# Linear attention and SwiGLU, forward and backward, on one core: a rebuilt k/q stage, six residual buffers and a bank-wise emptied dm step

## Chip, cores, metric

One core of one Trainium2 chip. The metric is device time in microseconds (us) of one execution of the whole kernel. The kernel before takes 821.44 us (median of 3 runs, 821.32 to 822.36).

Engines: PE is TensorE (matmuls), DVE is VectorE, ACT is ScalarE, POOL is GpSimd, SP issues most of the transfers. PE writes its results into the memory PSUM, and DVE or ACT copy them out. A *PSUM tile* is what the kernel allocates there at once; here each covers two *banks*. It is not to be confused with a tile of 128 rows. *By starts* means that a late start is measured as the start of an instruction less the end of PE's earlier work, counted with the usual distance from start to start (0.1355 us for a matmul of 320 columns).

## The reference, cut

```python
def _A_ref(x, wqkv, wo):                       # linear attention, 32 heads of 20
    q, k, v = ...                              # x @ wqkv, S = 2048, D = 640
    phi = lambda t: jnp.where(t > 0, t + 1, jnp.exp(t)) + 1e-6
    pq, pk = phi(q), phi(k)
    kv = jnp.einsum("bhsd,bhse->bhde", pk, v)
    z = jnp.einsum("bhsd->bhd", pk)
    ...                                        # o = (pq kv) / (pq z + 1e-6)
    return o @ wo
h = x + _A_ref(_layernorm(x), wqkv, wo)
h2 = h + (silu(_layernorm(h) @ w_gate) * (_layernorm(h) @ w_up)) @ w_down
# returned: h2 and the gradients of all inputs for a given grad_out
```

S is worked in 16 tiles of 128 rows. Three places matter here. The **k/q stage** (about 0 to 55 us) normalises each tile of x, transposes it on PE, multiplies by the k and q weights and forms phi. The **stage before h1** (about 85 to 100 us) builds W2, the product of the kv state with wo, and fills idle places of PE with "dm steps" (grad_out times the transposed w_down). The **h1 stage** (about 100 to 149 us) alternates products ps_a with dm steps; DVE adds x to ps_a. Names in the profile: xn is the normalised x and xnT its transposed copy, wqk are the k and q weights, rstd is the inverse root of the variance, ps_... are PSUM tiles, dm and dmst are the buffers into which ACT empties the dm steps, and ring is a buffer that transfers fill with dq and dk in the backward part.

## The kernel before, where the change touches it

```python
    def ln1(t):                                     # one tile: normalise, transpose, copy
        ...                                         # xn[:, t] on DVE (only centred for t < 2)
        tp = psum.tile([P, D], BF16, name="ps_t", tag="mm")
        for kt in range(DT):
            nc.tensor.transpose(tp[:, kt * P:(kt + 1) * P], xn[:, t, kt * P:(kt + 1) * P], ident[:])
        tpv = tp[:].rearrange("p (k c) -> p k c", c=P)
        if t == 0:
            wait_for(nc.scalar.copy(out=xnT[:, t, 0:3], in_=tpv[:, 0:3]), load_3())
            nc.scalar.copy(out=xnT[:, t, 3:5], in_=tpv[:, 3:5])
        else:
            nc.scalar.copy(out=xnT[:, t], in_=tpv)
    ...
    with tc.manual_schedule(engines={EngineType.PE, EngineType.DVE, EngineType.Activation}):
        ...
        warm(31)                                    # dummy matmuls until x lands
        ln1_stats(0)
        ...
        warm(12)
        ...
            if t + 2 < ST:                          # statistics two tiles ahead
                ln1_stats(t + 2)
                ln1_rstd(t + 2)                     # POOL: an addition and a power
        ...
    # the dm step: ten matmuls into both banks of one PSUM tile, one copy of both
                ps = mm("ps_dm")
                dm_mm(ps, wdT3 if g == 3 else wdT, t, g)
                dst = dmst[:, t // 2] if g == 3 else dm_t[g][:, t:t + 2, :]
                nc.scalar.copy(out=dst[:, :, :w], in_=ps[:, :, :w])
    ...
    # the stage before h1
        dm(1)
        for i in range(DT):
            if i == 3:
                dm(1)
            ps = mm("ps_w2t")
            mm_heads(ps, ...)
            nc.scalar.copy(out=half(W2T[:, i, :]), in_=row(ps))
            nc.sync.dma_start_transpose(out=W2[:, :, i * P:(i + 1) * P], in_=W2T[:, i, :])
        ...
        dm(3)
    # the h1 stage
        for t in range(ST + 2):
            if t < ST:
                xr = xrs.pop(t)                     # one of five buffers, loaded about two tiles ahead
                ps = mm("ps_a")
                mm_row(ps, ..., W2, ...)
                nc.vector.tensor_tensor(out=half(xr[:]), in0=row(ps), in1=half(xr[:]), op=ALU.add)
                ...
                dm(1)
            if t > 0:
                load_xr(t + 2)
            ...
            nc.scalar.dma_start(out=scr_h1_v[:, u, :], in_=h1[:])
```

`mm(name)` hands out one of four PSUM tiles, each of two banks. `manual_schedule` keeps the program's order on the engines that it names; POOL was not among them.

## Time and profile before

| | before |
|---|---|
| time, median (runs) | 821.44 us (3) |
| span of the profiled run | 819.0 us |
| PE busy | 812.0 us, 99% |
| first x lands (first statistics on DVE) | 3.62 us |
| tile 4's transposes | 18.31 us |
| z sums (end of the k/q stage) | 55.72 us |
| a dm step, and the one after it | 89.06, 92.10 us |
| first gate product pg (end of the h1 stage) | 149.12 us |

The table gives places on the time axis and not busy shares, because PE is busy almost all the time. A change can win only where PE's next instruction starts later than the one before it allows. The lines are in the prediction below.

### The profile page before, as it was taken

The page shows a single profiled execution, that of the slowest core. Times are in us where ns is not written, and L with a number is a line of the kernel's source. Part 1 is how long each engine was busy: PE and PEld are TensorE (multiplying, and loading weights), DVE is VectorE, ACT ScalarE, POOL GpSimd, SP SyncE. Part 2 cuts the span into 40 slices and gives each one's busy share as a digit, 9 for nine tenths or more (in the row PEclk, how much of TensorE's full clock was granted, in tenths as well). Part 3 has the DMA queues.
Part 4 walks back from the last instruction along what each step waited for, and adds up shares of the span by engine and source line. Part 5 has one row for each costly group of instructions (what it writes and reads, how often), then busy time and mean ns, then how long its engine had stood idle before and what let it go on. Part 6 is the DMA issues. An engine that isn't in the chain of part 4 may idle for free.

```text
span 819.0 us, 14057 instructions
## 1 busy us (share of the span) xinstructions
PE 812.0 (99%) x5540; PEld 521.7 (64%) x5540; DVE 442.4 (54%) x874; ACT 291.0 (36%) x412; POOL 188.2 (23%) x345
## 2 busy tenths in 40 slices
PE   8999999999999999999999999999999999999998
PEld 6776656555555555555566677777777777777675
DVE  6878676891077018810660147787793366631212
ACT  6982422770084126500741122322322133322010
POOL 3330022322412312221125301211220111112330
PEclk9999999999999999999999999999999999999999
DMA  9994589999759997894498757977498999999962
GB/s 301 195 356 86 140 175 280 244 226 214 198 123 206 208 207 178 183 249 115 98 233 185 258 123 217 219 206 181 110 224 178 172 174 165 176 204 259 227 177 75
DMA packets 278321, 158.61 MB, mean 194 GB/s; under 512 B 235052, under 2 KB 264877, under 8 KB 278256
## 3 DMA queue, kind: packets, MB, share of 16 engines
q1 hardware_dynamic: 251696, 82.12, 53.1%
q0 software_dynamic: 17744, 64.45, 26.6%
q10 hardware_dynamic: 8816, 11.16, 4.3%
q8 instruction: 43, 0.70, 0.4%
q14 instruction: 22, 0.18, 0.1%
HBM read 47.68 MB, written 53.66 MB: 124 GB/s over the span
## 4 chain that ended last, share of the span: by engine, by line
PE 92%; DVE 4%; ACT 2%; DMA 1%; issue 1%; POOL 0%; DVEq 0%; ACTq 0%
PE ps_dw L627 21%; PE ps_dhn L109 14%; PE ps_dxn L871 8%; PE ps_o L932 7%; PE pu L563 7%; PE pg L558 7%; PE ps_dwqk L109 5%; PE ps_dm L385 5%; PE ps_y L109 3%; PE ps_dp L109 3%; PE ps_dk L109 3%; PE ps_gt L678 3%; PE ps_a L109 3%; PE pdm L385 2%; DVE st L134 1%; ACT phi_e L307 1%
## 5 line engine op out<-in xcount | busy, mean ns | idle before, releaser
L109 PE MATMUL ps_dhn<-wgT,cols 128*128 128x320 bf16 x864 | 119.5, 299 | 0.0
L627 PE MATMUL ps_dw<-dd,hn 128*128 128x448 bf16 (+1 forms) x640 | 118.8, 346 | 0.0
L109 PEld LDWEIGHTS <-cols 128*128 128x128 bf16 x864 | 84.5, 98 | 32.9
L627 PEld LDWEIGHTS <-hn 128*128 128x128 bf16 x640 | 62.6, 98 | 54.2
L629 DVE CAST dwev<-ps_dw 128x896 bf16<-128x896 f32 (+3 forms) x12 | 10.9, 908 | 123.5 <-PE ps_dw L627 123.5
L629 ACT CAST dwev<-ps_dw 128x896 bf16<-128x896 f32 (+1 forms) x20 | 17.6, 878 | 157.9 <-PE ps_dw L627 146.7
L592 POOL DMA_DIRECT2D scr_dT<-stg x64 | 34.8, 543 | 168.7 <-DMA stg<-dd 163.2
L147 DVE CUSTOM_DVE_ANT_0 lb_a<-lb_dy,hn 128x640 bf16<-128x640 bf16 x32 | 26.4, 826 | 75.3 <-ACT lb_dy L145 75.3
L558 PE MATMUL pg<-wgu,hnT 128*128 128x448 bf16 (+1 forms) x320 | 63.6, 346 | 0.0
L563 PE MATMUL pu<-wgu,hnT 128*128 128x448 bf16 (+1 forms) x320 | 63.6, 346 | 0.0
L932 PE MATMUL ps_o<-wd,mT 128*128 128x320 bf16 (+3 forms) x462 | 61.3, 295 | 0.0
L627 PE MATMUL ps_dw<-m_s,dh 128*128 128x448 bf16 (+1 forms) x320 | 60.4, 346 | 0.0
L871 PEld LDWEIGHTS <-ring 128*128 128x128 bf16 x480 | 47.0, 98 | 18.2
L932 PEld LDWEIGHTS <-mT 128*128 128x128 bf16 (+1 forms) x462 | 41.8, 97 | 17.6 <-issue 2.6
L871 PE MATMUL ps_dxn<-wqkvT,ring 128*128 128x320 bf16 x320 | 51.3, 299 | 0.0
L563 PEld LDWEIGHTS <-hnT 128*128 128x128 bf16 x320 | 31.3, 98 | 27.1
L627 PEld LDWEIGHTS <-dh 128*128 128x128 bf16 x320 | 31.3, 98 | 27.1
L558 PEld LDWEIGHTS <-hnT 128*128 128x128 bf16 x320 | 31.3, 98 | 27.0
L298 PE MATMUL ps_kq<-wqk,xnT 128*128 128x320 bf16 x320 | 46.4, 299 | 1.4 <-ACT xnT L290 1.4
L385 PEld LDWEIGHTS <-dh2T 128*128 128x128 bf16 x320 | 31.1, 98 | 25.8 <-issue 0.9
L385 PE MATMUL ps_dm<-wdT,dh2T 128*128 128x448 bf16 (+1 forms) x240 | 46.8, 344 | 0.6 <-ACT dmst L399 0.5
L145 ACT ACTIVATE lb_dy<-ps_dhn,rstd 128x640 bf16<-128x640 f32 x16 | 12.7, 793 | 87.8 <-PE ps_dhn L109 87.8
(162 smaller groups left out, 1277.8 us busy)
## 6 DMA issues: line engine op xcount, KB each, us to landing
scr_dT<-stg POOLq DMA_DIRECT2D x48, 224.0 KB, 3.0
cols<-scr_dT POOLq DMA_DIRECT2D x6, 1728.0 KB, 8.1
scr_m<-m_s POOLq DMA_DIRECT2D x12, 448.0 KB, 4.4
cols<-scr_dT ACTq DMA_DIRECT2D x2, 1728.0 KB, 9.5
out_dram<-dwev POOLq DMA_DIRECT2D x30, 112.0 KB, 3.3
scr_dT<-stg POOLq DMA_DIRECT2D x16, 192.0 KB, 2.6
scr_pk<-pk SPq DMA_DIRECT2D x4, 640.0 KB, 7.5
scr_pq<-pqa SPq DMA_DIRECT2D x4, 640.0 KB, 7.8
```

The lines of the kernel that those rows point to most:

```text
L109: nc.tensor.matmul(ps[:, ci, :320], lhsT=lhs(k), rhs=rhs(k, *NCH[ci]), start=(start and k == 0), stop=(stop and k == n - 1))
L147: nc.vector.tensor_tensor_reduce(out=a[:], in0=dy[:], in1=xhat, scale=1.0, scalar=0.0, op0=ALU.mult, op1=ALU.add, accum_out=sums[:, 1:2])
L298: nc.tensor.matmul(ps[:, ci, :320], lhsT=xnT[:, t, k, :], rhs=wqk[:, k, w0 + n0:w0 + n1], start=(k == 0), stop=(k == DT - 1))
L385: nc.tensor.matmul(ps[:, c, :w], lhsT=dh2T[:, kt, (t + c) * P:(t + c + 1) * P], rhs=wdT[:, kt, o:o + w], start=(kt == 0), stop=(kt == DT - 1))
L558: nc.tensor.matmul(pg[:, c, :w], lhsT=hnT[:, kt, (t + c) * P:(t + c + 1) * P], rhs=wg[:, kt, 0:w], start=(kt == 0), stop=(kt == DT - 1))
L563: nc.tensor.matmul(pu[:, c, :w], lhsT=hnT[:, kt, (t + c) * P:(t + c + 1) * P], rhs=wg[:, kt, w:2 * w], start=(kt == 0), stop=(kt == DT - 1))
L592: nc.gpsimd.dma_start(out=scr_dT[t + c, :, KO[g]:KO[g] + GK[g], :], in_=stg[:, :GK[g], :])
L627: nc.tensor.matmul(ps[:, c, :w], lhsT=lhs(t), rhs=rhs(t), start=(t == 0), stop=(t == ST - 1))
L629: copy(out=ev[:, :len(parts), :w], in_=ps[:, :len(parts), :w])
L678: nc.tensor.matmul(ps[:, ci, :320], lhsT=dh1[:, t, i * P:(i + 1) * P], rhs=pqs_tm[:, t, n0:n1], start=(t == 0), stop=(t == ST - 1))
L871: nc.tensor.matmul(ps[:, ci, :320], lhsT=lhs[:, i, :], rhs=rhs[:, i, n0:n1], start=(k == 0 and i == 0), stop=(k == 2 and i == DT - 1))
L932: nc.tensor.matmul(po(t, ci), lhsT=mTs[t // 4][r, t % 4, j, :], rhs=wd[r, j, n0:n1], start=(t, ci) not in opened, stop=last)
```

## The change

The intent is to take away PE's remaining pauses: POOL's order and ACT's load at the start of the k/q stage, one wait for a PSUM buffer before h1, and late x in the h1 stage. The core of the diff, with cuts marked:

```diff
-    work = ctx.enter_context(tc.tile_pool(name="work", bufs=5))
+    work = ctx.enter_context(tc.tile_pool(name="work", bufs=6))
...
+    NC = 3
+    BY_V = (1, 2, 3, 6, 9, 12)          # tiles whose transposes DVE copies instead of ACT
...
+    def ln1_tr(t):                       # tiles 0 and 1: three transposes in one bank, two in the other
+        tp = psum.tile([P, 2, 2 * 512], BF16, name="ps_t", tag="mm")
+        for c, (k0, k1) in enumerate(((0, 3), (3, DT))):
+            for kt in range(k0, k1):
+                nc.tensor.transpose(tp[:, c, (kt - k0) * P:(kt - k0 + 1) * P], ...)
+        return [...]                     # one piece per bank
...
+        nc.scalar.activation(out=half(dst[:, t, :]), ..., func=ACT.Exp, scale=sc)
+        nc.scalar.activation(out=half(rr[...]), ..., func=ACT.Relu, scale=sc)
...
+    def phi(which, t, n=2):              # two tiles in one DVE operation
...
-    with tc.manual_schedule(engines={EngineType.PE, EngineType.DVE, EngineType.Activation}):
+    with tc.manual_schedule(engines={EngineType.PE, EngineType.DVE, EngineType.Activation, EngineType.Pool}):
...
+        ln1_centre(0, 0, 3 * P)          # first tile in pieces
+        ln1_centre(0, 3 * P, D)
+        copies(0, nc.scalar.copy)
+        warm(8)
...
+            kq_mm(t, 0, (lambda: copy1(t + 1)) if t + 1 < ST else None)
             if t == 2:
+                ln1_stats(4)
+                ln1_stats(5)
...
-                dm_mm(ps, wdT3 if g == 3 else wdT, t, g)
-                nc.scalar.copy(out=dst[:, :, :w], in_=ps[:, :, :w])
+                if g == 0 and t == 8:    # a copy after each half of the matmuls
+                    dm_mm(ps, wdT, t, g, lambda c: nc.scalar.copy(out=dst[:, c, :w], in_=ps[:, c, :w]))
+                else:
+                    dm_mm(ps, wdT3 if g == 3 else wdT, t, g)
+                    nc.scalar.copy(out=dst[:, :, :w], in_=ps[:, :, :w])
...
-        for t in range(3):
+        for t in range(6):
             load_xr(t)
...
-            if t > 0:
-                load_xr(t + 2)
+            if t > 2:
+                load_xr(t + 3)
```

More of the change, by code (lines that the diff above doesn't have):

```diff
@@ L174 @@
     wpool = wB.enter_context(tc.tile_pool(name="wpool", bufs=2))
+    fA = ExitStack()
+    rr = fA.enter_context(tc.tile_pool(name="fA", bufs=1)).tile([P, 4, 2, D], BF16, name="rr")
     def fw(name):
-        return wpool.tile([P, 2, GM], BF16, name=name, tag="f", bufs=6)
+        return fpool.tile([P, 2, GM], BF16, name=name, tag="f")
     def load_wgu(g):
@@ L258, with ln1_centre @@
     pqa = big.tile([P, ST, D], BF16, name="pqa", tag="B")
-    ers = {}
-    NC = 2
+    NC = 3
+    BY_V = (1, 2, 3, 6, 9, 12)
     def ln1_stats(t):
-        st = ln_stats(x_tm[t // 8][:, t % 8, :], mv1[:, t, :])
-        if t == 0:
-            wait_for(st, load_2())
+        st6 = small.tile([P, 2, 6], FP32, name="st6", tag="st6")
+        for ci, (n0, n1) in enumerate(NCH):
+            st = nc.vector.bn_stats(out=st6[:, ci, :], in_=x_tm[t // 8][:, t % 8, n0:n1])
+            if t == 0 and ci == 0:
+                wait_for(st, load_2())
+        nc.vector.bn_aggr(out=mv1[:, t, :], in_=st6[:].rearrange("p a b -> p (a b)"))
+        ln_rstd(mv1[:, t:t + 1, :], rstd1, t, 1)
+    def ln1_centre(t, c0=0, c1=D):
+        nc.vector.tensor_scalar(out=xn[:, t, c0:c1], in0=x_tm[t // 8][:, t % 8, c0:c1], scalar1=mv1[:, t, 0:1],
+                                scalar2=None, op0=ALU.subtract)
     def ln1_xn(t):
@@ L271, in ln1_xn, with ln1_tr1 @@
                                 scalar2=rstd1[:, t:t + 1], op0=ALU.subtract, op1=ALU.mult)
-    def ln1_rstd(t):
-        ln_rstd(mv1[:, t:t + 1, :], rstd1, t, 1)
-    def ln1(t):
-        if t < NC:
-            nc.vector.tensor_scalar(out=xn[:, t, :], in0=x_tm[t // 8][:, t % 8, :], scalar1=mv1[:, t, 0:1],
-                                    scalar2=None, op0=ALU.subtract)
-        else:
-            ln1_xn(t)
+    def ln1_tr(t):
+        tp = psum.tile([P, 2, 2 * 512], BF16, name="ps_t", tag="mm")
+        for c, (k0, k1) in enumerate(((0, 3), (3, DT))):
+            for kt in range(k0, k1):
+                nc.tensor.transpose(tp[:, c, (kt - k0) * P:(kt - k0 + 1) * P], xn[:, t, kt * P:(kt + 1) * P], ident[:])
+        return [(slice(k0, k1), tp[:, c, :(k1 - k0) * P].rearrange("p (k c) -> p k c", c=P))
+                for c, (k0, k1) in enumerate(((0, 3), (3, DT)))]
+    def ln1_tr1(t):
         tp = psum.tile([P, D], BF16, name="ps_t", tag="mm")
@@ L284, in ln1, with kq_mm @@
             nc.tensor.transpose(tp[:, kt * P:(kt + 1) * P], xn[:, t, kt * P:(kt + 1) * P], ident[:])
-        tpv = tp[:].rearrange("p (k c) -> p k c", c=P)
-        if t == 0:
-            wait_for(nc.scalar.copy(out=xnT[:, t, 0:3], in_=tpv[:, 0:3]), load_3())
-            nc.scalar.copy(out=xnT[:, t, 3:5], in_=tpv[:, 3:5])
-        else:
-            nc.scalar.copy(out=xnT[:, t], in_=tpv)
-    def kq_mm(t, which, between=None):
+        return tp[:].rearrange("p (k c) -> p k c", c=P)
+    def kq_mm(t, which, between=None, pieces=((0, DT),)):
         dst, w0 = ((pk, D), (pqa, 0))[which]
         ps = mm("ps_kq")
-        for k0, k1 in ((0, 3), (3, DT)) if t == 0 else ((0, DT),):
+        for k0, k1 in pieces:
             for ci, (n0, n1) in enumerate(NCH):
@@ L299, in kq_mm @@
                                      start=(k == 0), stop=(k == DT - 1))
-            if between and (t > 0 or k0 == 0):
+            if between and k0 == 0:
                 between()
-        def act():
-            e = fw("phi_e")
-            r = fw("phi_r")
-            sc = rstd1[:, t:t + 1] if t < NC else 1.0
-            nc.scalar.activation(out=e[:, :, :320], in_=row(ps), func=ACT.Exp, scale=sc)
-            nc.scalar.activation(out=r[:, :, :320], in_=row(ps), func=ACT.Relu, scale=sc)
-            ers.setdefault(t, []).append((dst, e, r))
@@ L311, in kq_mm @@
-        return act
-    def kq_phi(t, last=True):
-        n = len(ers[t]) if last else 1
-        for _ in range(n):
-            dst, e, r = ers[t].pop(0)
-            nc.vector.tensor_scalar(out=e[:, :, :320], in0=e[:, :, :320], scalar1=1.0, scalar2=1e-6,
-                                    op0=ALU.min, op1=ALU.add)
-            nc.vector.tensor_tensor(out=half(dst[:, t, :]), in0=e[:, :, :320], in1=r[:, :, :320], op=ALU.add)
-        if last and t % 4 == 3:
-            sl = slice(t - 3, t + 1)
-            nc.sync.dma_start(out=scr_pk_v[:, sl, :], in_=pk[:, sl, :])
-            nc.sync.dma_start(out=scr_pq_v[:, sl, :], in_=pqa[:, sl, :])
-            nc.sync.dma_start(out=scr_xnT[sl].rearrange("t p k c -> p t k c"), in_=xnT[:, sl])
@@ L326 @@
-    with tc.manual_schedule(engines={EngineType.PE, EngineType.DVE, EngineType.Activation}):
+        sc = rstd1[:, t:t + 1] if t < NC else 1.0
+        nc.scalar.activation(out=half(dst[:, t, :]), in_=row(ps), func=ACT.Exp, scale=sc)
+        nc.scalar.activation(out=half(rr[:, 2 * which + t // 2 % 2, t % 2, :]), in_=row(ps), func=ACT.Relu, scale=sc)
+    def phi(which, t, n=2):
+        e = (pk, pqa)[which][:, t:t + n, :]
+        nc.vector.tensor_scalar(out=e, in0=e, scalar1=1.0, scalar2=1e-6, op0=ALU.min, op1=ALU.add)
+        nc.vector.tensor_tensor(out=e, in0=e, in1=rr[:, 2 * which + t // 2 % 2, t % 2:t % 2 + n, :], op=ALU.add)
+        if (t + n) % 4 == 0:
+            sl = slice(t + n - 4, t + n)
+            if which == 0:
+                nc.sync.dma_start(out=scr_pk_v[:, sl, :], in_=pk[:, sl, :])
+            else:
+                nc.sync.dma_start(out=scr_pq_v[:, sl, :], in_=pqa[:, sl, :])
+                nc.sync.dma_start(out=scr_xnT[sl].rearrange("t p k c -> p t k c"), in_=xnT[:, sl])
@@ L328 @@
+    PIECES = ((0, 3), (3, DT))
+    with tc.manual_schedule(engines={EngineType.PE, EngineType.DVE, EngineType.Activation, EngineType.Pool}):
         ps = mm("ps_warm")
@@ L332, in warm, with copies, copy1 @@
                 nc.tensor.matmul(ps[:, 0, :P], lhsT=ident[:], rhs=ident[:], start=True, stop=True)
+        def copies(t, eng_copy):
+            for sl, src in ln1_tr(t):
+                c = eng_copy(out=xnT[:, t, sl], in_=src)
+                if t == 0 and sl.start == 0:
+                    wait_for(c, load_3())
+        def copy1(t):
+            (nc.vector.tensor_copy if t in BY_V else nc.scalar.copy)(out=xnT[:, t], in_=ln1_tr1(t))
         warm(31)
         ln1_stats(0)
-        ln1_rstd(0)
@@ L337 @@
-        ln1(0)
-        warm(12)
+        ln1_centre(0, 0, 3 * P)
+        ln1_centre(0, 3 * P, D)
+        copies(0, nc.scalar.copy)
+        warm(8)
         ln1_stats(1)
-        ln1_rstd(1)
-        kq_mm(0, 0, lambda: ln1(1))()
+        ln1_centre(1)
+        kq_mm(0, 0, lambda: copies(1, nc.vector.tensor_copy), PIECES)
         ln1_stats(2)
-        ln1_rstd(2)
-        kq_mm(1, 0)()
-        kq_mm(0, 1)()
-        for t in range(1, ST):
-            if t == 1:
-                ln1(2)
-            if t > 1:
-                kq_mm(t, 0, (lambda: ln1(t + 1)) if t + 1 < ST else None)()
-            if t == 2:
-                kq_phi(0)
-            if t + 2 < ST:
-                ln1_stats(t + 2)
-                ln1_rstd(t + 2)
-            if t == 1:
-                kq_phi(0, last=False)
-            kq_mm(t, 1)()
-            if t > 1:
-                kq_phi(t - 1)
-            if t >= ST - NC:
-                ln1_xn(t - ST + NC)
@@ L363 @@
-        kq_phi(ST - 1)
+        ln1_centre(2)
+        kq_mm(1, 0, None, PIECES)
+        ln1_stats(3)
+        kq_mm(0, 1, lambda: copy1(2), PIECES)
+        phi(0, 0)
+        ln1_xn(3)
+        kq_mm(1, 1)
+        for t in range(2, ST):
+            if t > 3 and t + 3 < ST:
+                ln1_stats(t + 3)
+            kq_mm(t, 0, (lambda: copy1(t + 1)) if t + 1 < ST else None)
+            if t == 2:
+                ln1_stats(4)
+                ln1_stats(5)
+            if t == 3:
+                ln1_stats(6)
+            if t == ST - 1:
+                phi(0, t - 1, 1)
+            kq_mm(t, 1)
+            if t == 3:
+                phi(1, 0)
+            elif t == ST - 1:
+                phi(0, t, 1)
+                phi(1, t - 3)
+                phi(1, t - 1)
+            elif t > 3:
+                phi(t % 2, t - 2 - t % 2)
+            if t + 2 < ST:
+                ln1_xn(t + 2)
+            if ST - NC - 1 <= t < ST - 1:
+                ln1_xn(t - ST + NC + 1)
@@ L375, with dm_mm @@
         ps_z = mm("ps_zb")
+    fA.close()
+    fpool = wB.enter_context(tc.tile_pool(name="fpool", bufs=6))
     dm_t = {0: strips.tile([P, ST, GM], BF16, name="dm0", tag="S")}
-    def dm_mm(ps, wdT, t, g):
+    def dm_mm(ps, wdT, t, g, each=None):
         w = GW[g]
@@ L386, in dm_mm @@
                                  rhs=wdT[:, kt, o:o + w], start=(kt == 0), stop=(kt == DT - 1))
+            if each:
+                each(c)
     def dm_steps():
@@ L396, in dm_steps @@
                 ps = mm("ps_dm")
-                dm_mm(ps, wdT3 if g == 3 else wdT, t, g)
                 dst = dmst[:, t // 2] if g == 3 else dm_t[g][:, t:t + 2, :]
-                nc.scalar.copy(out=dst[:, :, :w], in_=ps[:, :, :w])
+                if g == 0 and t == 8:
+                    dm_mm(ps, wdT, t, g, lambda c: nc.scalar.copy(out=dst[:, c, :w], in_=ps[:, c, :w]))
+                else:
+                    dm_mm(ps, wdT3 if g == 3 else wdT, t, g)
+                    nc.scalar.copy(out=dst[:, :, :w], in_=ps[:, :, :w])
                 if g == 3:
```

## The prediction

> **What bounds the kernel now.** I read the page first, then who waited for whom on TensorE (PE), then the timelines of the engines by start times over the first 150 us.
>
> Page, parts 1 and 4 (chain of waits):
>
> ```profile
> span 819.0 us, 14057 instructions
> PE 812.0 (99%) x5540; PEld 521.7 (64%) x5540; DVE 442.4 (54%) x874; ACT 291.0 (36%) x412; POOL 188.2 (23%) x345
> ...
> PE 92%; DVE 4%; ACT 2%; DMA 1%; issue 1%; POOL 0%; DVEq 0%; ACTq 0%
> ```
>
> PE is busy 812.0 of 819.0 us. The change removes no matmul that counts (four warm-up ones), so it can only win the time in which PE stands still. Who PE waited for:
>
> ```profile
> PE ps_warm L332 <- POOL ident masks.py:199: 1.4, 1, 1.4
> PE ps_kq L298 <- ACT xnT L290: 1.4, 2, 1.1
> PE ps_dm L385 <- ACT dmst L399: 0.5, 1, 0.5
> PE ps_t L284 <- DVE xn L278: 0.3, 1, 0.3
> PE ps_z L370 <- DVE pk L319: 0.2, 1, 0.2
> ```
>
> 3.8 us in all, 1.4 of it the preamble, which stays. The ends of matmuls are modelled (a matmul of 320 columns is shown as 299 ns, yet the next one starts after 135), so gaps under about 0.16 us are hidden and shown gaps are that much too short. I therefore measure gaps from start to start. The PE timeline of the k/q stage:
>
> ```profile
> 6.25 0.99 PE L298 MATMUL ps_kq<-wqk,xnT 128*128 128x320 bf16 x6
> 7.08 0.44 PE L284 MATMUL ps_t<-ident,xn 128*128 128x128 bf16 x5
> 7.36 0.71 PE L298 MATMUL ps_kq<-wqk,xnT 128*128 128x320 bf16 x4
> 8.31 2.89 PE L298 MATMUL ps_kq<-wqk,xnT 128*128 128x320 bf16 x20 [0.24 <-ACT xnT L290]
> 11.03 0.44 PE L284 MATMUL ps_t<-ident,xn 128*128 128x128 bf16 x5
> 11.31 1.52 PE L298 MATMUL ps_kq<-wqk,xnT 128*128 128x320 bf16 x10
> 13.95 1.53 PE L298 MATMUL ps_kq<-wqk,xnT 128*128 128x320 bf16 x10 [1.12 <-ACT xnT L290]
> 15.32 0.44 PE L284 MATMUL ps_t<-ident,xn 128*128 128x128 bf16 x5
> 15.60 2.88 PE L298 MATMUL ps_kq<-wqk,xnT 128*128 128x320 bf16 x20
> 18.31 0.44 PE L284 MATMUL ps_t<-ident,xn 128*128 128x128 bf16 x5
> ```
>
> From 15.60 to 18.31 are 20 matmuls: 135.5 ns each. Five transposes take 0.28. A tile so costs PE 2.99 us, and from 15.32 to 51.27 the transposes repeat every 2.99 to 3.00 us: **PE never waits in the steady part**. The trap is that ScalarE (ACT) shows no idle time there either (five operations, starts 3.00 us apart from tile to tile), and VectorE (DVE) needs 3.01 us per tile. Three engines are matched, and the chain of waits names ACT's phi_e and phi_r. Lightening ACT and DVE cannot shorten a stage whose PE work already lies end to end. What is open is the start: 7.36 + 4 x 0.1355 = 7.90 to 8.31 is 0.41, and 11.31 + 1.355 = 12.67 to 13.95 is 1.28. The cause of both shows on POOL and ACT:
>
> ```profile
> 8.49 1.62 POOL L140 TENSOR_TENSOR rstd<-lnv,nhalf 128x1 f32<-128x1 f32 x3
> 9.10 0.79 ACT L307 ACTIVATE phi_e<-ps_kq,rstd 128x640 bf16<-128x640 f32 x1 [0.85 <-POOL rstd L140]
> 13.17 0.72 ACT L290 COPY xnT<-ps_t 128x640 bf16<-128x640 bf16 x1
> ```
>
> POOL did the additions of tiles 0, 1 and 2 before its first power, so the first phi began at 9.10 though its matmuls were done at about 7.9; ACT never caught up, and the copy of tile 2 went behind six phi operations at 13.17.
>
> Two later places, same method. In the stage before h1, PE's w2t products end at 90.95 + 21 x 0.043 = 91.85 (0.043 from 14 of them between 93.99 and 94.59) and the next dm step starts at 92.10: 0.25. In the stage of ps_a and dm, a ps_a product starts 0.19 late at 116.71, and the dm step at 137.19 comes 0.70 after 135.14 + 1.355. There DVE waits for x:
>
> ```profile
> 115.83 0.82 DVE L513 TENSOR_TENSOR xr<-ps_a,xr 128x640 bf16<-128x640 f32 x1 [3.62 <-DMA xr<-in_A_x_dram]
> 127.19 0.82 DVE L513 TENSOR_TENSOR xr<-ps_a,xr 128x640 bf16<-128x640 f32 x1 [2.43 <-DMA xr<-in_A_x_dram]
> 136.34 0.80 ACT L399 CAST dmst<-ps_dm 128x768 bf16<-128x768 f32 x1 [4.33 <-DVE hn L530]
> ```
>
> Late x makes DVE late; ACT issues the h1 stores in order, stands behind them, and empties dm late.
>
> **What the Trainium skill says.** (1) "Trainium Kernel Development and Optimization", Performance Expectations: matmul busy time is a bad metric since matmuls are pipelined. The trace agrees: 299 ns shown against 135.5 from start to start. (2) "TensorE: Matmul & The Clock Gate", "Wait — 56ns, not 53.3ns?": a warm matmul takes N / 2.4 GHz plus about 2.5 ns, which is 135.8 for 320 columns and 55.8 for 128. Measured 135.5 and 56: PE is at its floor. (3) "VectorE: DVE Perf Modes", the errata section's table and "Why PSUM operands drop a tier": a copy out of PSUM costs 120 + FD/Accel cycles at 0.96 GHz, with at most two elements a cycle for 16-bit data. I estimate 0.46 us for 640 elements, 0.33 for 384 and 0.26 for 256. The trace of before has no such copy; fp32 ones of 896 elements on DVE take 0.91 to 1.09, in keeping with one element a cycle. (4) "PSUM — Partial Sum Buffer", PSUM bank collisions: guard PSUM by bank. Splitting the transposes, and the dm step, over two banks lets the first bank be read while PE writes the second.
>
> **The change, part by part.** I walked the new program order through the four engines with the durations above (DVE: statistics 0.92 + 0.13, centring 0.30, normalising 0.36 from start to start; ACT with a per-row scale 0.68 an operation, without 0.59; from the start of the aggregate to a usable rstd 1.46, as at 11.41 to 12.87).
>
> *First tile in pieces.* DVE centres 384 columns in about 0.22 instead of 640 in 0.30, so the transposes start near 5.10 instead of 5.23; ACT's copy waits for three of them, not five (0.11). First k matmul at 6.0 instead of 6.25: gain 0.24. The next x and the q weights are asked for after the first half of the statistics, about 0.65 earlier, so weights (3.8 us to landing) are there by 8.4, before the 9.0 at which q starts.
>
> *Order of POOL, copies on DVE.* POOL in program order has rstd of tile 0 by about 6.2. Phi of tile 0 starts when its matmuls end, near 7.9. DVE's two copies of tile 1 (7.2 to 7.8) let k of tile 1 follow at 7.66 without the gap of 0.41. Then q of tile 0 from 9.0, q of tile 1 from 10.7, k of tile 2 from 12.0: the gap of 1.28 is gone too, since DVE copied tile 2 at 10.3. So far PE is 0.24 + 0.41 + 1.28 = 1.9 ahead: tile 4's transposes would be due at 16.4, not 18.31.
>
> *Statistics ahead: a new wait.* The program puts the statistics of tiles 4 and 5 behind the DVE copy of tile 3, which has to await tile 3's transposes (13.4 + 0.5). Copy to 14.25, statistics 4: aggregate starts at 15.17, statistics 5 to 16.35, rstd of tile 4 at 15.17 + 1.46 = 16.63, and PE sees xn about 0.45 later, at 17.1. PE was ready at 16.4. So I expect one new wait of about 0.7, on tile 4's transposes, which gives back a third: **net gain of the start 1.2**. Later the tiles clear by 0.4 us or more each, since joint phi (about 1.29 for two tiles against 2 x 0.79 = 1.58) brings DVE under 2.7 us a tile.
>
> *Six copies on DVE (3.5 us of ACT) and joint phi (0.15 us of DVE per tile):* beside PE's work; worth 0 in the steady part. The end of the stage stays: phi of tile 15 waits for ACT's relu, and 0.2 stays on the z sums.
>
> *dm step by bank:* the first half is copied while PE fills the second; the buffer is free about 0.36 before 92.06. Gain 0.25, all of that gap.
>
> *Six x buffers:* tiles 3 to 5 are loaded before the SP queue is taken by the transposes of pq (until 112.6), later ones three tiles ahead, some 6 to 9 us against a landing of 3.2 (at most 6.4). Both gaps go: 0.19 + 0.70 = 0.89; I book 0.85.
>
> Sum 1.2 + 0.25 + 0.85 = **2.3 us** (the roundings taken together). After 150 us PE lies end to end, so the gain should reach the end undiminished: 821.44 - 2.3 = 819.1 us.
>
> **Rivals.** (A) *ACT is the bound of the k/q stage*, as its unbroken row and the chain's phi_e and phi_r suggest. Six copies of 0.59 gone would then shorten the stage by 3.5 us in place of 1.2, and the kernel would land near 816.8. Against it: PE's 135.5 ns and 2.99 us a tile leave nothing to take. (B) *No new wait on tile 4*: if rstd or DVE's copies are quicker than I reckon, the start yields its full 1.9 and the kernel lands at 818.4. For it: POOL's power varies from 0.54 to 0.82 us. (C) *The freed waits come back as others*: a queue of transfers that is nearly full from 120 to 180 us (mean share 1.07 or more) could make x late in spite of its third tile of lead, or the tracking of the one shared buffer of relu results could tie ACT's writes to DVE's reads. Then only 0.5 to 1 us is left, 820.5 or more. Against it: the k/q stage's buffers are reused after four tiles, and x moves out of the crowded stretch.
>
> **Range and chances.** The start between 0.6 and 1.9, dm 0.1 to 0.25, x 0.4 to 0.9; with B and the good ends 818.3, with the bad ends 820.3. Runs of before spread by 1 us. Range 818.0 to 820.4, centre 819.1. 2% is 16 us, more than twice all idle time of PE, so faster by over 2% gets 0.01; slower would need a wait of 16 us, 0.01.
>
> **What would show it.** In the changed profile: first k matmul near 6.0; no ACT-caused gap before 14; a PE wait on xn of tile 4 of about 0.7 near 17; transposes 2.99 us apart after it; tile 15's z sums about 1.2 earlier; the dm step right behind the w2t products; no DVE wait for x above 1 us and no late start of PE between 100 and 148. Wrong would be: a shorter period than 2.99 (rival A), no wait at 17 (B), or new gaps after 20 us (C).

## The result

The kernel after takes **820.23 us** (median of 4 runs, 819.70 to 820.97) against 821.38 in the same session (4 runs, 821.25 to 822.36). The ratio is 0.9984 with a 95% interval of 0.9967 to 1.0001. Ratios here are the mean time of one kernel's runs over that of the other's of the same rounds, so not quite the ratio of the medians quoted. The gain is about 1.15 us where 2.3 was predicted. The interval just includes 1, so these eight runs alone do not show a gain clear of noise; the repeat e12 below, with 0.9988 [0.9976, 1.0000], points the same way. The class "within 2%" and the range 818.0 to 820.4 held.

Page of the kernel after, parts 1 and 4:

```profile
span 817.9 us, 13973 instructions
PE 811.4 (99%) x5536; PEld 521.1 (64%) x5536; DVE 443.5 (54%) x853; ACT 288.9 (35%) x407; POOL 191.5 (23%) x345
...
PE 97%; ACT 1%; DVE 1%; DMA 0%; issue 0%; DVEq 0%
```

The span fell by 1.1 us and the chain of waits now runs over PE for 97% where it had 92%. Who PE waited for, after (columns: us in total, times, longest):

```profile
PE ps_warm L330 <- POOL ident masks.py:199: 1.4, 1, 1.4
PE ps_t L286 <- DVE xn L275: 0.7, 1, 0.7
PE ps_dm L406 <- ACT dm L422: 0.6, 1, 0.6
PE ps_t L293 <- DVE xn L279: 0.3, 1, 0.3
PE ps_z L388 <- DVE pk L313: 0.2, 1, 0.2
```

The two waits of the first lines of the k/q stage (ps_kq for ACT's xnT, 1.4 us) and the one on dmst are gone. Two are new: a dm step waits for ACT's copy of its own first half (L422 is the new bank-wise copy), and transposes wait for xn (L279 is the normalising). The start of PE's timeline shows the latter (columns: start, duration, engine, line, operation, count, idle time shown before it and its releaser):

```profile
7.48 2.96 PE L302 MATMUL ps_kq<-wqk,xnT 128*128 128x320 bf16 x20
10.28 0.44 PE L293 MATMUL ps_t<-ident,xn 128*128 128x128 bf16 x5
10.72 3.51 PE L302 MATMUL ps_kq<-wqk,xnT 128*128 128x320 bf16 x24
14.06 0.44 PE L293 MATMUL ps_t<-ident,xn 128*128 128x128 bf16 x5
14.34 2.88 PE L302 MATMUL ps_kq<-wqk,xnT 128*128 128x320 bf16 x20
17.57 0.45 PE L293 MATMUL ps_t<-ident,xn 128*128 128x128 bf16 x5 [0.35 <-DVE xn L279]
```

By the starts of the single matmuls the gap of 0.41 is down to 0.07 (before tile 1's k, at 8.10), and the one of 1.28 is gone. From 14.34 twenty matmuls last to 14.34 + 20 x 0.1355 = 17.05, but tile 4's transposes start at 17.57: a new wait of 0.52. DVE's timeline shows why:

```profile
14.55 0.49 DVE L339 COPY xnT<-ps_t 128x640 bf16<-128x640 bf16 x1 [1.55 <-PE ps_t L293]
14.95 0.88 DVE L268 BATCH_NORM_STATS2 st<-x_tm 128x6 f32<-128x320 bf16 x2
...
17.07 0.45 DVE L279 TENSOR_SCALAR xn<-x_tm,mv,rstd 128x640 bf16<-128x640 bf16 x1
```

DVE stood idle 1.55 us for tile 3's transposes before it could start the statistics of tile 4, as the prediction walked it. From tile 5 on the period is 2.99 to 3.00 us, as before.

The stage before h1, PE, in the kernel before:

```profile
89.06 2.05 PE L385 MATMUL ps_dm<-wdT,dh2T 128*128 128x448 bf16 x10
...
92.10 2.05 PE L385 MATMUL ps_dm<-wdT,dh2T 128*128 128x448 bf16 x10
```

and after, PE and then the first of ACT's two copies:

```profile
88.33 1.10 PE L406 MATMUL ps_dm<-wdT,dh2T 128*128 128x448 bf16 x5
90.05 1.11 PE L406 MATMUL ps_dm<-wdT,dh2T 128*128 128x448 bf16 x5 [0.62 <-ACT dm L422]
91.00 1.04 PE L128 MATMUL ps_w2t<-yk,wvo 128*128 128x120 bf16 x21
91.89 2.05 PE L406 MATMUL ps_dm<-wdT,dh2T 128*128 128x448 bf16 x10
```

```profile
89.47 0.53 ACT L422 CAST dm<-ps_dm 128x448 bf16<-128x448 f32 x1 [1.58 <-PE ps_dm L406]
```

The first five matmuls (0.19 each, from ten of them between 89.06 and 90.95 before) are issued by 89.28. The second five start at 90.05, right after ACT's copy of the first half ended at 90.00. PE lost 0.77 in the middle of the step. The aim of the change was met all the same: the next dm step comes right after the w2t products (91.00 + 21 x 0.043 = 91.90). From one dm step to the next it took 3.04 before and 3.56 after.

In the h1 stage DVE no longer waits for x at all (7.8 us in four waits before). Its wait on the adding of x is now for PE:

```profile
DVE xr L539 <- PE ps_a L109: 9.2, 12, 0.9
```

From the dm step at 92.10 (91.89 after) to the first gate product at 149.12 (148.02) it took 57.02 before and 56.13 after: 0.89 gained.

The sum, in this pair of traces: start of the k/q stage +0.74 (z sums at 54.98, not 55.72), dm step -0.52, h1 stage +0.89, together 1.11, which is the difference of the spans. Behind 149 us everything is shifted by that amount.

### The profile page after: what moved, and what is told of

It is laid out like the page before. It is cut to its first block, busy times and chain, and to the rows that moved or that the text cites. A ratio compares the mean times of both kernels' runs of the same rounds, so it can differ in the third digit from the quotient of the medians.

```text
span 817.9 us, 13973 instructions
## 1 busy us (share of the span) xinstructions
PE 811.4 (99%) x5536; PEld 521.1 (64%) x5536; DVE 443.5 (54%) x853; ACT 288.9 (35%) x407; POOL 191.5 (23%) x345
## 4 chain that ended last, share of the span: by engine, by line
PE 97%; ACT 1%; DVE 1%; DMA 0%; issue 0%; DVEq 0%
PE ps_dw L653 21%; PE ps_dhn L109 14%; PE ps_dxn L897 8%; PE ps_o L958 7%; PE pg L584 7%; PE pu L589 7%; PE ps_dwqk L109 5%; PE ps_dm L406 5%; PE ps_kq L302 4%; PE ps_y L109 3%; PE ps_dk L109 3%; PE ps_gt L704 3%; PE ps_a L109 3%; PE ps_dp L109 3%; PE pdm L406 2%; ACT rr L308 1%
```

## The experiments

Twelve runs were made, in three sessions, with the kernel before beside each. The second session was on another chip of the same type than the first and the third. The kernel before had a median of 820.95 in the first session (e1 to e4), of 821.37 in the second (e5 to e8, where two of its seven runs were at 823.4 and 826.3, so that the intervals are wide) and of 820.83 in the third. The time differences looked for are mostly below the spread between runs of one kernel (1 us and more), so the times are given as a check. All outputs were correct.

**e1: the dm step in one copy again.**

```diff
-                if g == 0 and t == 8:
-                    dm_mm(ps, wdT, t, g, lambda c: ...copy of bank c...)
-                else: ...
+                dm_mm(...); nc.scalar.copy(out=dst[:, :, :w], in_=ps[:, :, :w])
```

> The changed kernel with the dm step of tiles 8 and 9 emptied in one copy again, as before. Theory: the program makes the second half's matmuls wait for ScalarE's copy of the first half, because the wait is set for the whole PSUM tile and not for the bank; so the split costs time. From that dm step's first matmul to the next dm step's first matmul: 3.04 us as in the kernel before, against 3.56 in the changed kernel; nothing else moves; about 0.5 us off the whole, near 819.7. Rival: the pause has another cause (ScalarE late, weights late) and only showed there: then 3.5 us or so stays and the time stays at 820.2.

Measured: 820.05 us (819.45 to 820.63), ratio 0.9990 [0.9975, 1.0005]. From dm step to the next 3.05 (88.57 to 91.62), and no pause inside the step: the split had caused the 0.77. "Nothing else moves" missed: to the gate product it takes 59.75 from the dm step, against 59.69 in the kernel after, so that nothing of the 0.51 came through. A new wait showed up 10 us later:

```profile
101.02 0.85 PE L109 MATMUL ps_a<-wvo,pqsT 128*128 128x320 bf16 x5 [0.40 <-DMA wvo<-wvo]
```

The second half of the first ps_a product needs the last piece of the transposed W2, which five transposes in a row on SP's queue deliver. By starts it is 101.02 - 99.78 - 5 x 0.1355 = 0.56 late. PE came there earlier without the pause, but that is the smaller part of it. The transposes themselves were slower in this trace:

```profile
92.19 7.35 SPq L522 DMA_TRANSPOSE wvo<-wvo  x5
```

They took 7.35 us, against 6.88 in the kernel after. With 6.88 W2 would have been about 0.1 late (an estimate: 0.56 - 0.47). In all traces with three dm steps ahead of ps_a they took 7.00 to 7.50 where W2 was late (e1, e2, e7, e9, e12) and 6.48 to 6.97 where it was in time. What makes them slower in one run than in another is left open.

**e2: each half of the dm step in a PSUM tile of its own.**

```diff
+                    for c in range(2):
+                        pc = ps if c == 0 else mm("ps_dm")
+                        ...five matmuls into pc[:, 0, :w]...
+                        nc.scalar.copy(out=dst[:, c, :w], in_=pc[:, 0, :w])
```

> The same step by halves, but each half in a PSUM tile of its own, so that no matmul has to wait for a copy of the other half. Theory: the pause inside the step goes and the buffer is free in time too, so the distance from this step's first matmul to the next step's is the bare work, 10 x 0.189 + 21 x 0.043 = 2.79 us; 0.77 us less than the changed kernel, near 819.5. Rival: with one PSUM buffer more in use another wait on a buffer appears, and 3.0 us or more stays.

Measured: 819.40 us (819.26 to 820.70), ratio 0.9985 [0.9970, 1.0000].

```profile
88.40 2.05 PE L425 MATMUL ps_dm<-wdT,dh2T 128*128 128x448 bf16 x10
...
91.18 2.05 PE L406 MATMUL ps_dm<-wdT,dh2T 128*128 128x448 bf16 x10
```

The same work with the same two copies and no pause: 2.78 to the next dm step, PE's own work. So the pause comes from the shared PSUM *tile*, not from reading one bank while the other is written. The list of semaphore waits in the built program of the kernel after says the same: the first matmul into the second bank waits for the count that ACT's copy of the first bank raises. The wait for W2 is there again (0.46 by starts); the transposes took 7.36 us in this trace, and with 6.88 W2 would have been in time (the same estimate: 0.46 - 0.48).

**e3: statistics of tile 4 ahead of DVE's copy of tile 3.**

```diff
+            if t == 2:
+                ln1_stats(4)
             kq_mm(t, 0, (lambda: copy1(t + 1)) ...)
             if t == 2:
-                ln1_stats(4)
                 ln1_stats(5)
```

> The changed kernel with the statistics of tile 4 placed ahead of VectorE's copy of tile 3 (they stood behind it). Theory: PE's wait on the normalised tile 4 (0.52 us from start to start) comes from that order, so it goes; tile 4's transposes start 5 x 0.056 + 20 x 0.1355 = 2.99 us after tile 3's in place of 3.51; 0.5 us off the whole, near 819.7. Rival: the wait is set by GpSimd's inverse root, not by the order on VectorE, or tile 3's copy is now late and the wait only moves to the next matmul: then 3.4 to 3.5 us stays.

Measured: 819.54 us (819.27 to 820.90), ratio 0.9987 [0.9972, 1.0002]. Tile 3's to tile 4's transposes took 3.00 (14.28 to 17.28) in place of 3.51, and the wait for xn of tile 4 left the list:

```profile
17.28 0.44 PE L293 MATMUL ps_t<-ident,xn 128*128 128x128 bf16 x5
```

The program order is the cause, as the prediction said.

**e4: the kernel after with five x buffers, loaded as before.**

```diff
-    work = ctx.enter_context(tc.tile_pool(name="work", bufs=6))
+    work = ctx.enter_context(tc.tile_pool(name="work", bufs=5))
...and load_xr for three tiles at first, then for t + 2...
```

> The changed kernel with five work buffers, three early loads of x and two tiles of lead, as before. Theory: the loads of x alone account for the gain in the stage of ps_a and dm, so the stretch from the dm step after the first w2t products to the first gate product goes back from 56.13 to 57.0 us, with waits of VectorE on x of 2 us and more; 0.9 us more than the changed kernel, near 821.1. Rival: the stage gained because it starts at another phase to the transfers; then the stretch stays within 0.3 us of 56.1.

Measured: 820.36 us (820.06 to 821.62), ratio 0.9997 [0.9980, 1.0014]. From the later dm step to the gate product 56.35, against 56.13 after and 57.02 before. DVE waits for x as long as ever:

```profile
DVE xr L539 <- DMA xr<-in_A_x_dram: 7.0, 4, 3.2
```

yet PE lost only 0.22 by it (at 136.55). The theory's 0.9 missed; the stretch stayed within the rival's 0.3 of 56.1. The rival's reason, that the stage meets the transfers at another phase, was not tested by itself.

**e5 and e9: the kernel before with POOL in program order and nothing else, twice.**

```diff
-    with tc.manual_schedule(engines={EngineType.PE, EngineType.DVE, EngineType.Activation}):
+    with tc.manual_schedule(engines={EngineType.PE, EngineType.DVE, EngineType.Activation, EngineType.Pool}):
```

> The kernel before with one word more: GpSimd too keeps the program's order in the k/q stage, so the inverse root of tile 0 is no longer queued behind the variance additions of tiles 1 and 2. Theory A: this order alone is what the start gained; ScalarE's first phi starts near 8.0 to 8.3 instead of 9.1, everything on ScalarE up to the copy of tile 2 moves by that, PE's gap of 1.28 us before 13.95 shrinks to about 0.4, and from the landing of the first x to tile 4's transposes it takes about 13.9 us, like the 13.8 of the changed kernel, against 14.7 before. Theory B: the copies on VectorE and the statistics ahead are what counts; then the gap stays above 1 us and the stretch above 14.5.

Measured in e5: 821.41 us (820.32 to 821.86), ratio 0.9986 [0.9954, 1.0017]. The profiled run does not settle it, because the first matmuls ran at half rate:

```profile
7.40 1.80 PE L298 MATMUL ps_kq<-wqk,xnT 128*128 128x320 bf16 x6
9.00 0.74 PE L284 MATMUL ps_t<-ident,xn 128*128 128x128 bf16 x5
```

Six matmuls took 1.60, 0.267 each, where 0.1355 is the usual. The full rate came at about 9.9. Therefore the repeat:

> Same kernel as e5 (the kernel before with GpSimd in program order and nothing else), repeated because TensorE ran at half rate at the start of e5's profiled run. Theory (the order on GpSimd caused most of the two early gaps): from the landing of x to tile 4's transposes about 13.9 us, against 14.69 in the kernel before (18.31 less 3.62), so about 0.8 less: the gap before tile 2's k falls from 1.28 to about 0.4 to 0.7, the one of 0.41 before tile 1's k (bank copies) stays. Rival (the gaps come from ScalarE doing all copies and phi in order, and the order on GpSimd matters little): the gap before tile 2's k stays above 1.0 and the sum at 14.5 or more. Time about 820.6 against 821.4.

Measured in e9: 820.48 us (820.18 to 820.87), ratio 0.9993 [0.9980, 1.0006].

```profile
13.76 1.53 PE L298 MATMUL ps_kq<-wqk,xnT 128*128 128x320 bf16 x10 [0.52 <-ACT xnT L290]
```

Its ten matmuls before began at 11.72 and were through at 13.08, so the gap before tile 2's k is 0.68 in place of 1.28; the gap of 0.41 before tile 1's k stays (8.24 to 8.64). From the landing of x (3.96) to tile 4's transposes (18.13) it is 14.17, against 14.69 before and 13.79 after. POOL's order alone is worth about 0.5 of the 0.9 that the k/q stage gained; it is less than the theory's 0.8 and more than the rival's 0.2. The rest came with the other parts, which were not run one by one. In e5 and e9 another thing shows: both load x as the kernel before does, DVE waits 9 us for it in both, and yet PE loses almost nothing by it: what the dm step and W2 leave of its late starts is 0.03 in e5 and 0.02 in e9.

**e6: all copies back on ACT.**

```diff
-    BY_V = (1, 2, 3, 6, 9, 12)
+    BY_V = ()
```

(Tile 1's two pieces stay on DVE.)

> The changed kernel with all copies of xnT from tile 2 on given back to ScalarE (tile 1 stays on VectorE). Theory: PE's own work sets the period of 2.99 us, so the period does not change although ScalarE has five operations per tile again; and since VectorE need not await the transposes of tile 3 before the statistics of tile 4, PE's wait of 0.52 on tile 4 goes: about 0.5 us less than the changed kernel, near 819.6. Rival: ScalarE is the bound of the stage, as the chain of waits of the kernel before suggests; the five moved copies of 0.6 us each come back and the time is 821 to 823.

Measured: 820.69 us (819.78 to 821.84), ratio 0.9975 [0.9938, 1.0012]; the profiled run again had the half-rate start, so its beginning is not used. Later the tiles follow at 3.00 us as in the kernel after, and from tile 4's transposes to the z sums it is 37.48 against 37.41. ACT with all copies does not bound the stage: rival A falls. (The time, 820.69, is neither the theory's 819.6 nor the rival's 821 to 823.) And without DVE's copy of tile 3 tile 4's transposes come 3.00 after tile 3's: the copies given to DVE made the new wait.

**e7: the kernel before with six x buffers only.**

```diff
-    work = ctx.enter_context(tc.tile_pool(name="work", bufs=5))
+    work = ctx.enter_context(tc.tile_pool(name="work", bufs=6))
...and load_xr for six tiles at first, then for t + 3...
```

> The kernel before with the six x buffers and their earlier loads alone. From the first matmul of the dm step of tiles 8 and 9 to the first gate product it took 60.06 us before and 59.69 in the changed kernel, 59.75 with the step in one copy. Theory: the loads of x take away the two late starts (0.19 and 0.70), but PE then reaches the last piece of the transposed W2 some 0.4 us before it has landed, so only part is left: 59.7 to 59.8, a wait of 0.3 to 0.5 us on that transfer, and 0.3 us off the whole, near 820.7. Rival, my prediction's reckoning: nothing takes its place, 59.2 us.

Measured: 821.07 us (820.67 to 826.11), ratio 0.9997 [0.9955, 1.0040]. No late start from x. From the dm step to the gate product 59.39 against 60.06 before; W2 was 0.22 late here (it was in time before). That lies between the theory's 59.7 to 59.8, which reckoned with W2 0.3 to 0.5 late, and the rival's 59.2.

**e8: e1 and four dm steps ahead of the ps_a products, not three.**

```diff
-        dm(3)
+        dm(4)
```

> The changed kernel with the dm step of tiles 8 and 9 in one copy, and one dm step more ahead of the first ps_a product (four in a row in place of three, one less later). Theory: the transposes of W2 bound the start of ps_a; with 1.89 us more of other work ahead of it the wait of 0.4 us on them is gone, and the stretch from that dm step to the first gate product falls from 59.75 to about 59.2 us (the gap of 0.25 on the buffer stays); 0.5 us less than the run with one copy, 0.5 less than the changed kernel. Rival: the wait has to do with the transfers' load and comes back elsewhere, or the last two ps_a products without a dm step between them wait for VectorE: 59.6 or more.

Measured: 819.47 us (819.45 to 820.19), ratio 0.9966 [0.9935, 0.9997]. The wait for W2 is gone and the gate product comes 59.17 after the dm step, as the theory had it. The transposes took 6.88 us here, so W2 would not have been very late anyway. The better test of the added step is e11 below: there they took 7.66, the longest of all, and nothing waited.

**e10: the kernel after with four edits** (the dm halves of e2, the statistics of e3, the dm(4) of e8, and the first tile's transposes in two PSUM tiles):

```diff
+        if t == 0:
+            for k0, k1 in ((0, 3), (3, DT)):
+                tp = psum.tile([P, 2 * 512], BF16, name="ps_t", tag="mm")
+                ...transposes k0 to k1 into tp, one piece each...
```

**e11** is e10 with `warm(36)` in place of `warm(31)`; **e12** is the kernel after, unchanged, as a base in the same rounds.

> The kernel after with four edits: first tile's transposes in two PSUM tiles, statistics of tile 4 ahead of the copy of tile 3, dm step's halves in two PSUM tiles, four dm steps before the ps_a products in place of three. Theory: ScalarE's first copy starts about 0.39 after the first transposes (0.51 in the kernel after); tile 3 to tile 4 transposes 3.00 (3.51 after); dm step to the next 2.78 (3.56 after); no wait for the transposed W2; from the dm step to the first gate product about 58.9 (59.69 after). Sum 0.1 + 0.5 + 0.8 = 1.4 us less than the kernel after, so about 818.8 median. Rival (the waits removed come back elsewhere, as in e1): dm step to gate product 59.4 or more and 819.4 or more.

> e10 with 36 warm-up products in place of 31, so that TensorE idles 0.3 to 0.5 us less before the first transposes. Theory (the spread of 1 to 1.3 us between runs of one kernel is TensorE falling back to half rate when it stood idle between the warm-up and the first transposes): runs with the slow start become rarer, the highest of the runs within 0.6 us of the lowest. Rival (the spread comes from the arrival of x or of the weights, or from when the warm-up begins against a fixed window): the spread stays at 1 us or more, median as in e10.

> The kernel after unchanged, as a base on the same chip and in the same rounds for e10 and e11. Expected: 819.7 to 821.0, ratio to the kernel before 0.9984 to 0.9986, dm step to gate product 59.69, tile 3 to 4 transposes 3.5, dm step to the next 3.56. With it the theory for e10 says 1.4 us between the two medians, the rival 0.8 or less.

Measured, five rounds each:

| | median, us | range (runs) | ratio to before |
|---|---|---|---|
| e10 | 818.84 | 818.51 to 821.06 (6) | 0.9976 [0.9963, 0.9990] |
| e11 | 819.10 | 818.40 to 820.09 (5) | 0.9975 [0.9963, 0.9987] |
| e12 (after) | 819.95 | 819.87 to 820.95 (5) | 0.9988 [0.9976, 1.0000] |

The four edits are worth about 1 us (1.11 and 0.85 by the medians, 1.36 and 1.47 by the fastest runs), against 1.4 expected (the rival: 0.8 or less). Three of them did in both traces what was expected: tile 3 to tile 4 takes 2.99 and 3.00; dm step to dm step 2.78; no wait for W2. The fourth shows in e11, where ACT's first copy starts 0.38 after the first transposes, not 0.51 (in e10 the transposes themselves were slow, 0.71 shown for five, so nothing can be read off). In e11 the gate product comes 58.91 after the dm step, as expected and the shortest of all. In e10's profiled run (819.46, one of its slower ones) it is 59.72, because of a wait in another place:

```profile
134.27 1.78 PE L414 MATMUL ps_dm<-wdT,dh2T 128*128 128x384 bf16 x10 [0.64 <-ACT dmst L438]
```

ACT emptied a dm buffer late. It issues the h1 stores in order with its copies, and there one store was issued only at 133.04. Why it was held so long in this run is left open; e8, with the same h1 stage, had no such wait.

The warm-up theory behind e11 fell: the runs still spread by 1.7 us. And e12's profiled run, slower than its four others by 1.0, had an ordinary start (1.05 from the transposes to the first k, and its six matmuls in 0.82, as in the kernel after) and this instead, late in the backward part:

```profile
PE ps_dxn L897 <- DMA ring<-dq: 1.0, 1, 1.0
```

So in this slow run a transfer landed late, and the wait for it is of just the size of the difference; the four others were not profiled. Waits for such a ring transfer cost 0.5 in e6 and 0.2 in e1. A slow start, late W2, and a late ring transfer each come and go between runs of one kernel.

**What each late start cost.** By starts on PE, from the dm step to the first gate product; 58.91 is e11's, taken as PE's work end to end:

| trace | inside or behind the dm step | W2 late | dm buffer or x late | sum | measured less 58.91 |
|---|---|---|---|---|---|
| before | 0.25 | 0 | 0.89 | 1.14 | 1.15 |
| after | 0.77 | 0 | 0 | 0.77 | 0.78 |
| after, again (e12) | 0.77 | 0.22 | 0 | 0.99 | 1.00 |
| e1, one copy | 0.26 | 0.56 | 0 | 0.82 | 0.84 |
| e2, two tiles | 0 | 0.46 | 0 | 0.46 | 0.48 |
| e4, five x buffers | 0.77 | 0 | 0.22 | 0.99 | 1.00 |
| e7, six x buffers alone | 0.25 | 0.22 | 0 | 0.47 | 0.48 |
| e8, one copy, dm(4) | 0.25 | 0 | 0 | 0.25 | 0.26 |
| e9, before, POOL in order | 0.25 | 0.37 | 0 | 0.62 | 0.64 |
| e10 | 0 | 0 | 0.81 | 0.81 | 0.81 |

The rows close to 0.03. (The first column is the time to the next dm step less 2.79; the second and third are starts less the end of the matmuls before.)

## Why the prediction was right in class and half wrong in size

- **The range held, partly by luck.** 820.23 lies 0.17 inside its slow end. The dm step fell outside the 0.1 to 0.25 given for it; that the total stayed inside is owed to x, which came at its good end in the two traces compared (see below). The class said little: 2% is 16 us. (A slip: with B and the good ends the sum is 821.44 - 1.9 - 0.25 - 0.9 = 818.4, not 818.3.)
- **What bounds it.** Right. PE at 135.5 ns a matmul and 2.99 to 3.00 us a tile stayed so in every trace with and without the copies on ACT (e6). Rival A is refuted.
- **"dm step by bank: ... Gain 0.25, all of that gap."** This is the step that failed, with the wrong sign: -0.52 in place of +0.25, a miss of 0.77 that makes up most of the 1.2 missing. The 0.25 was gained, as the next dm step shows, but the second half of the split step waits for ACT's copy of the first. The prediction argued from PSUM banks: the Trainium skill, "PSUM — Partial Sum Buffer", PSUM bank collisions, says to guard by bank, and no trace here contradicts that for the hardware. But the waits in a built program are set by what this kernel allocates as one tile. e2, with two tiles, has no pause; e1 has none without the split.
- **"First tile in pieces: ... gain 0.24."** Measured 0.03 (first k 2.63 after the landing of x before, 2.60 after). The centring in pieces gave 0.06 of the 0.13 reckoned, and the copy gave nothing. Of the latter the cause is the same: ACT's copy of the three transposes in the first bank waits in the built program for the fifth transpose, so it starts 0.51 after the first one against 0.49 before. With two tiles it is 0.38 (e11). Besides, x landed at 3.78 in place of 3.62, which is 0.16 lost to no one's doing.
- **Weights "there by 8.4".** Wrong. They were asked for 0.5 earlier than before (4.7 and 5.7, not 5.2 and 6.2), but took 4.7 and 5.0 us to land, not 3.8 and 4.1, and so came at 9.4 and 10.7, no earlier than before. The second piece of tile 0's q so began 0.15 late, at 10.72. In e11, which starts earlier against x, they landed at 9.8 and 11.2, and PE is shown waiting for them (0.39 shown, 0.63 by starts, and 0.24 for the second piece): their landing is the next limit of the start.
- **Gaps of 0.41 and 1.28.** All but 0.07 of the two is gone, as predicted. POOL's order alone takes away 0.6 of the 1.69 (e9). Not foreseen were two small ones, the 0.15 on the weights and 0.09 before tile 1's q.
- **"A new wait of about 0.7 on tile 4's transposes."** Right in place and cause (e3), 0.52 in size.
- **Start, net 1.2.** 0.74: 1.69 of gaps gone, less 0.52 and 0.31 (0.07, 0.15 and 0.09) new or left, plus 0.03, less the 0.16 of late x, is 0.73.
- **Six x buffers, 0.85.** 0.89 between the two traces, but this hit is partly luck. Three other traces with the old loading show 0.22, 0.03 and 0.02 lost to x (e4, e5, e9), although DVE waits 7 to 9 us for x in each. With six buffers PE lost nothing to x in any trace (in e12 DVE waited for it once, 0.9). The step that was mis-sized is "Both gaps go": in the direct test, e4, the loads account for 0.22; that they gave the other 0.67 is not shown. The one trace of before lost more than the three others with the old loading, and e4 and e7 give no clear difference in time.
- **Rival C, the freed waits come back as others**, held in a form that the prediction did not name: not x nor relu results, but the dm step's own copy, and in some runs the transposed W2 (0.22 to 0.56 in e1, e2, e7, e9 and e12).
- **"After 150 us PE lies end to end".** True in the two traces compared; not in every run (e12's 1.0, e6's 0.5).
- **Other numbers of the skill.** "VectorE: DVE Perf Modes": the estimate of 0.46 for a copy of 640 bf16 elements out of PSUM agrees with the 0.44 and 0.49 measured. One reading was off: the 0.91 for fp32 copies of 896 elements on DVE is a mean over several shapes; that shape alone takes 1.09 (six copies).

## What to carry to other kernels

Splitting an operation so that another engine may start on its first half pays only if the program's dependencies are that fine: give each half its own buffer, and look in the built program or in the next trace at what the second half waits for. A wait on a side engine, however long, is not by itself a cost; measure it by late starts of the engine that is the bound, and in more than one run, since 0.9 us in one trace was 0 to 0.2 in three others. When a pause is taken away, ask what lands just behind it: here a transposed weight was in time in some runs and late by up to 0.56 us in others, and an independent step moved ahead of it took that up.

## What the Trainium skill lacked or had wrong

- "PSUM — Partial Sum Buffer", PSUM bank collisions: it gives the bank as the unit to guard (more finely, a quadrant of a bank), but does not say that in a kernel built from tiles the waits go by the allocated tile. One tile over two banks cost 0.77 us in a dm step and 0.13 us on the first transposes; two tiles cost nothing (e2, e11). No page consulted for this states the unit of tracking.
- "TensorE: Matmul & The Clock Gate", What's actually happening: it gives a state of 1.2 GHz with a window that runs free of the kernel, and so a variable start. The runs agree: 0.267 us for 320 columns in e5 is 320 / 1.2 GHz, until about 9.9 us. It does not spell out that a warm-up of 31 matmuls from 1.42 us on may fail so: the profiled runs of e5 and e6 ran at half rate until about 9.9 us, while the profile's row of the granted clock, whose slices are some 20 us long, showed 9 throughout. The page's free-running window of 3.4 us could explain it (an estimate from that figure: a window that ends at 9.9 began at 6.5, and the one before it held PE's pause from 4.7 to 5.6); no run tests this. Five more warm-up matmuls did not narrow the spread of times (e11, 1.7 us).
- Nothing on how much the landing of a transfer varies between runs of one kernel was found: the first x arrived between 3.62 and 4.09 us after the start, the five transposes of W2 took 6.48 to 7.66 us, W2 was 0 or 0.22 us late in two traces of the same kernel, and a late ring transfer cost 0 or 1.0 us.
